# Middle experts of a mixture layer in pairs of PSUM banks: accumulation on TensorE, 768-column operations, differences read from PSUM

## The chip, the cores and the metric

One Trainium2 chip, of which the kernel uses one core. The metric is the device time of one execution in microseconds (us). Before the change it was 2509.31 us (median of three runs, 2509.23 to 2515.71). The core's engines work in parallel, each on its own queue in order: TensorE (PE) multiplies into PSUM, whose 2 KB banks hold 512 fp32 columns for each of 128 partitions; VectorE (DVE) and ScalarE (ACT) read and write PSUM and SBUF; GpSimd (POOL) works on SBUF alone; SyncE (SP) issues most transfers. They wait for each other by semaphores.

## The reference

Three stages follow one another, all in fp32: a linear attention, a soft mixture of eight experts over its 2304 tokens of width 512, and a second mixture that sends every token to one expert. The change is in the first mixture:

```
x: 2304 x 512      w1: 8 x 512 x 1024      w2: 8 x 1024 x 512
P = exp(x @ w_gate - max), then 8 rounds of normalising its rows and its columns
for e in range(8):
    h = maximum(x @ w1[e], 0)
    out += P[:, e:e+1] * (h @ w2[e])
```

## The kernel before, in words

Everything is kept transposed, features on partitions and tokens along the columns. A matmul's operand is split in a high part, rounded to a shorter mantissa, and the rest (tile[:, 0] and tile[:, 1]), and a product is made of high x high, high x rest and rest x high: three matmuls for each 128 rows (`product`, lines 412 to 417).

The hidden width of an expert is cut in halves, so there are 16 half experts n, and the tokens in three blocks bi of 768; `HS` lists the 48 pairs (n, bi) in the order in which they run, with the blocks up and down in turn, so that two neighbours of a change of n have the same tokens. Each pair, which the text calls a block, is a 2 x 2 by 2 x 2 block product for layer 1 (x by w1) and another for layer 2 (h by w2), over quarters of 384 tokens. Both are done by Strassen's scheme in Winograd's form, with 7 products in place of 8. In the code, S1 to S4 are the sums of weight quarters, T1 to T4 those of the moving side (of x, and of h in layer 2), A11 to A22 weight quarters, B11 to B22 moving ones. A product has two output halves j, of six matmuls of 128x384 each.

Blocks with n below 2 and with n = 15 run the seven products in layer 1 alone, and plain products in layer 2 (`p2_plain`). The 39 blocks with n from 2 to 14 (the mixed ones) run seven products in both.

Layer 1 (`p1_group`, line 491) goes through the seven products for j = 0 and then for j = 1, each into a bank of 384 columns: m = A11 B11 is copied to SBUF by ScalarE (`tu`), u = m + S2 T2 and v = u + S1 T1 (`tv`) are added by VectorE, S4 B22 goes into the same bank as S1 T1, and so on; each of the four results then goes through `put`. In a mixed block `put` is `strassen` (line 457): VectorE takes the maximum with 0 and multiplies by the gate, writing SBUF; then come the layer-2 sums T1 to T4 (`comb`, line 462), the high parts by ScalarE (`high`, line 428) and the rests (`rest`, line 431). For j = 0 the sums and rests are GpSimd's, for j = 1 VectorE's; all of these have their operands in SBUF. `later` delays some by a number of ticks. Layer 2 (`p2_strassen`, line 765) then runs S4, A11, S3, S1, S2, A12 and A22; behind each j of each product VectorE adds the bank to the block's running sum in SBUF (`acc`, line 768).

The order of the work is written out by hand. Each generator yields after a piece of some six matmuls; a yield is a tick, and `at_tick(h, i, fn)` hangs other work on tick i of block h: the seven reloads of the next block's x tiles (`xreload`, ticks 7 to 13), the load of the next gates (`load_gate`, tick 16) and, in the third block of a half expert, the preparation of the next half's weights (`wops`): two raw loads a layer, four sums of 128x512 on GpSimd, and for each of seven weights a high part by ScalarE (line 338) and a rest by GpSimd (line 339).

Of the kernel before, what the change touches and what calls it, by code (L numbers as in the profile page):

```python
# [25 lines left out]
P = 128  # L26
# [13 lines left out]
XUSE = ("B11", "T2", "T1", "B22", "T3", "B21", "T4")  # L40
# [5 lines left out]
def build(tc, a, out):  # L46
# [4 lines left out]
    pp = top.enter_context(tc.tile_pool(name="pp", bufs=1, space=PSUM))  # L51
# [39 lines left out]
    live = {}  # L91
# [327 lines left out]
    hb, pend = {}, deque()  # L419
    HN = {(0, 0): "B11", (0, 1): "T1", (1, 0): "B21", (1, 1): "B22"}  # L420

    def raw_h(nm, j):
        t = live["h3"].tile([P, TH], F32, tag="r" + {"B22": "T2", "B21": "T4"}.get(nm, nm), bufs=1 if nm in ("B11", "T3") else 2, name="r" + nm)
        hb["raw", nm, j] = t
        return t

    def high(nm, j, src=None):
        A.copy(hb[nm][:, 0, j], hb["raw", src or nm, j])  # L428

    def rest(nm, j, eng, src=None):  # L430
        eng.tensor_tensor(out=hb[nm][:, 1, j], in0=hb["raw", src or nm, j], in1=f32(hb[nm][:, 0, j]), op=ALU.subtract)  # L431

    def later(ticks, fn, *args):
        pend.append([ticks, partial(fn, *args)])

    def pending():
        for x in list(pend):
            x[0] -= 1
            if x[0] < 0:
                pend.remove(x)  # L440
                x[1]()
# [6 lines left out]
    def gate(nm, j, th, src):  # L448
        V.scalar_tensor_tensor(out=raw_h(nm, j), in0=src, scalar=0.0, in1=hb["gate"][:, th * TH:(th + 1) * TH], op0=ALU.max, op1=ALU.mult)  # L449

    def gated(hv, th, j, src):
        nm = HN[hv, th]
        gate(nm, j, th, src)
        high(nm, j)
        later(1, rest, nm, j, V if j else G)

    def strassen(hv, th, j, src):
        eng, dl = (V, 0) if j else (G, 2)

        def comb(out, x, y):  # L460
            o = hb["raw", out, j] if ("raw", out, j) in hb and out != "T3" else raw_h(out, j)
            eng.tensor_tensor(out=o, in0=hb["raw", x, j], in1=hb["raw", y, j], op=ALU.subtract)  # L462

        if (hv, th) == (0, 1):
            gate("T1", j, 1, src)
        elif (hv, th) == (1, 1):
            gate("T2", j, 1, src)
            high("B22", j, "T2")
            comb("T3", "T2", "T1")
            rest("B22", j, eng, "T2")  # L470
            later(dl, high, "T3", j)
            later(dl + 1, rest, "T3", j, eng)
        elif (hv, th) == (0, 0):
            gate("B11", j, 0, src)
            comb("T1", "T1", "B11")
            high("B11", j)
            comb("T2", "T2", "T1")
            rest("B11", j, eng)
            later(dl, high, "T1", j)
            later(dl + 1, rest, "T1", j, eng)  # L480
            later(dl, high, "T2", j)
            later(dl + 2, rest, "T2", j, eng)
        else:
            gate("T4", j, 0, src)
            high("B21", j, "T4")
            later(0, rest, "B21", j, eng, "T4")
            later(0, comb, "T4", "T2", "T4")
            later(dl + 1, high, "T4", j)
            later(dl + 2, rest, "T4", j, eng)

    def p1_group(n):
# [3 lines left out]
        put = plain if n < 2 else gated if n == NGR - 1 else strassen  # L495
        for nm in ("B11", "T1", "B21", "B22"):
            hb[nm] = hp.tile([P, 2, 2, TH], F32R, tag="h" + nm, name=f"h{nm}")
        if put is strassen:
            for nm in ("T2", "T3", "T4"):
                hb[nm] = live["h3"].tile([P, 2, 2, TH], F32R, tag="h" + nm, name=f"h{nm}")  # L500
        if n >= 2:
            hb["gate"] = gates.popleft()
        for j in range(2):
            b0 = psum("A", [P, TH])
            product(b0, 1, j, "A11", xs["B11"], True, True)
            tu = hp.tile([P, TH], F32, tag="tu", name="tu")
# [8 lines left out]
            tv = hp.tile([P, TH], F32, tag="tv", name="tv")  # L515
# [8 lines left out]
            add(tv, b2, tv)  # L524
            put(1, 1, j, tv)
# [239 lines left out]
    def p2_strassen(n, bi):  # L765
        def read(q_, j, ps, op=ALU.add):
            z = acc(bi)[:, q_, j]
            V.tensor_tensor(out=z, in0=z, in1=ps, op=op)  # L768

        Y = [psum("A", [P, TH]) for _ in range(2)]  # L770
        for k in range(2):
            for j in range(2):
                product(Y[j], 2, j, "S4", hb["B22"], True, True, (k,))
                if k:
                    read(1, j, Y[j], ALU.subtract)
            yield

        def both(banks, wn, hn, start, q_, op=ALU.add):
            for j in range(2):
                product(banks[j], 2, j, wn, hb[hn], start, True)  # L780
                read(q_, j, banks[j], op)
                yield

        X = [psum("D", [P, TH]) for _ in range(2)]
        yield from both(X, "A11", "B11", True, 0)
        yield from both(Y, "S3", "T3", False, 3)
        Z = [psum("A", [P, TH]) for _ in range(2)]
        yield from both(Z, "S1", "T1", True, 1)
        yield from both(X, "S2", "T2", False, 1)
        W_ = [psum("D", [P, TH]) for _ in range(2)]  # L790
        yield from both(W_, "A12", "B21", True, 0)
        yield from both(Z, "A22", "T4", False, 2, ALU.subtract)

# [223 lines left out]
    def pair(which, j, nm):  # L1017
# [12 lines left out]
    def wsplit(i, which, c):  # L1030
        r = rw[which][c]
        j = n_w[which] % 7
        n_w[which] += 1
        hi, lo = pair(which, j, f"{i}_{c}")
# [121 lines left out]
    SL15 = {"A21": "S3"}  # L1156
    for h, (n, bi) in enumerate(HS):
        nxt = HS[h + 1][1] if h + 1 < NH else bi
        if nxt != bi:
            if n:  # L1160
                for k in range(len(XUSE)):
                    at_tick(h, 7 + k, partial(xreload, nxt, k))
# [254 lines left out]
```

## Time and profile before

| | |
|---|---|
| median of three runs | 2509.31 us |
| the profiled execution, its span | 2515.74 us, 2513.9 us |
| PE busy | 2123.5 us (84%) |
| DVE busy | 1616.5 us (64%) |
| POOL busy | 1164.6 us (46%) |
| ACT busy | 857.3 us (34%) |
| mean granted TensorE clock | 0.925 |

The busy time of PE counts matmuls from start to modelled end, and they overlap, so it overstates how full TensorE is. The granted clock is a share of the full 2.4 GHz; it has two levels, 1.2 and 2.4 GHz, so a value between them is a mix over the stretch. In the rows below, psA and psD are PSUM banks, xB and xT the tiles of x, hB and hT those of the gated h, rB and rT their unsplit values, w1A to w2S the weights, acca and accb the running sums. L417 is line 417.

### The profile page before, as it was taken

The numbers are of one execution on the slowest core, as the hardware profiler recorded it, in microseconds if no ns is written. First come the engines' busy times: TensorE is split into PE (matmuls) and PEld (weight loads), VectorE is DVE, ScalarE is ACT, GpSimd is POOL, SyncE is SP. The second block draws the span as 40 slices with busy tenths as digits, with TensorE's granted clock in tenths as the row PEclk, the third lists the DMA queues.
The fourth block names the chain that finished last, engine by engine and source line by source line (L and its number), as shares of the span: only waits on it lengthen the run. The fifth ranks groups of instructions, "written<-read, shape, count | busy, mean of one in ns | idle before, by whom it ended". The sixth has DMA issues, their size and how long they took to land.

```text
span 2513.9 us, 32723 instructions
## 1 busy us (share of the span) xinstructions
PE 2123.5 (84%) x11627; PEld 1984.8 (79%) x11627; DVE 1616.5 (64%) x2740; ACT 857.3 (34%) x1625; POOL 1164.6 (46%) x1036
## 2 busy tenths in 40 slices
PE   9999999878787878787878787878787878689998
PEld 9998888778686868777777777878786878577887
DVE  6665454666666666666656665666666563459996
ACT  5564321222222222222222223131313122267776
POOL 1263223555555555546463637282827241126553
PEclk9999999998898989898989898989898988889999
DMA  3344533323232424151505141423333225535472
GB/s 114 116 161 156 205 124 112 128 95 134 99 141 91 162 75 171 64 197 32 205 24 205 39 190 60 169 79 149 115 114 132 98 97 123 92 51 176 160 244 101
DMA packets 128313, 314.43 MB, mean 125 GB/s; under 512 B 20856, under 2 KB 75272, under 8 KB 128146
## 3 DMA queue, kind: packets, MB, share of 16 engines
q1 hardware_dynamic: 124050, 301.79, 35.2%
q0 software_dynamic: 4096, 10.51, 1.5%
q8 instruction: 93, 1.52, 0.3%
q14 instruction: 74, 0.61, 0.1%
HBM read 335.78 MB, written 32.05 MB: 146 GB/s over the span
## 4 chain that ended last, share of the span: by engine, by line
PE 53%; DVE 23%; POOL 11%; ACT 4%; DMA 4%; issue 4%; SPq 1%; DVEq 0%; POOLq 0%; ACTq 0%
PE psA L415 10%; PE psA L417 8%; PE psA L416 8%; DVE rT L462 4%; DVE rT L449 4%; PE psD L415 3%; PE psD L417 3%; PE psD L416 3%; DVE hB L431 3%; DVE tv L493 3%; DVE psA L493 3%; POOL hT L431 2%; PE psD L200 2%; ACT hB L428 2%; DVE hT L431 2%
## 5 line engine op out<-in xcount | busy, mean ns | idle before, releaser
L462 POOL TENSOR_TENSOR rT<-rT,rT 128x384 f32<-128x384 f32 x117 | 118.8, 1015 | 687.8 <-DVE rT L449 681.7
L415 PE MATMUL psD<-hB,w2A 128*128 128x384 f32 x528 | 194.0, 367 | 93.2 <-ACT hB L428 73.2
L428 ACT CAST hT<-rT 128x384 fp32r<-128x384 f32 x318 | 161.4, 512 | 224.2 <-POOL rT L462 106.8
L415 PE MATMUL psA<-hT,w2S 128*128 128x384 f32 x312 | 138.1, 443 | 110.2 <-DVE acca L768 71.9
L431 POOL TENSOR_TENSOR hT<-rT,hT 128x384 fp32r<-128x384 f32 x159 | 194.3, 1246 | 53.6 <-ACT hT L428 53.6
L416 PE MATMUL psD<-hB,w2A 128*128 128x384 f32 x528 | 193.9, 367 | 22.5 <-DVE hB L431 22.5
L493 DVE TENSOR_TENSOR psA<-psA,tu 128x384 f32<-128x384 f32 x192 | 108.1, 563 | 150.6 <-PE psA L417 150.2
L415 PE MATMUL psA<-xT,w1S 128*128 128x384 f32 x576 | 195.4, 339 | 2.0 <-DVE hB L446 2.0
L417 PE MATMUL psA<-xT,w1S 128*128 128x384 f32 x576 | 194.2, 337 | 0.0
L416 PE MATMUL psA<-xT,w1S 128*128 128x384 f32 x576 | 193.9, 337 | 0.0
L428 ACT CAST hB<-rT 128x384 fp32r<-128x384 f32 x156 | 80.2, 514 | 332.9 <-DVE rT L449 332.9
L507 ACT COPY tu<-psA 128x384 f32<-128x384 f32 x96 | 45.7, 476 | 432.9 <-PE psA L417 432.7
L417 PE MATMUL psD<-hB,w2A 128*128 128x384 f32 x528 | 188.8, 358 | 0.0
L415 PEld LDWEIGHTS psD<-hB,w2A 128*128 128x128 f32 x528 | 108.0, 205 | 100.0 <-ACT hB L428 77.4
L415 PEld LDWEIGHTS psA<-hT,w2S 128*128 128x128 f32 x312 | 81.9, 263 | 125.1 <-DVE acca L768 81.6
L768 DVE TENSOR_TENSOR acca<-acca,psA 128x384 f32<-128x384 f32 x208 | 112.6, 551 | 93.0 <-PE psA L417 93.0
L493 DVE TENSOR_TENSOR tu<-psA,tu 128x384 f32<-128x384 f32 x96 | 53.5, 557 | 137.2 <-PE psA L417 76.6
L415 PE MATMUL psA<-xB,w1S 128*128 128x384 f32 x192 | 75.4, 393 | 77.5 <-DVE tv L493 74.5
L416 PEld LDWEIGHTS psD<-hB,w2A 128*128 128x128 f32 x528 | 108.0, 205 | 36.0 <-DVE hB L431 36.0
L416 PE MATMUL psA<-hT,w2S 128*128 128x384 f32 x312 | 133.1, 426 | 0.0
L417 PE MATMUL psA<-hT,w2S 128*128 128x384 f32 x312 | 131.8, 423 | 0.0
L415 PE MATMUL psA<-xB,w1A 128*128 128x384 f32 x384 | 130.6, 340 | 0.0
(372 smaller groups left out, 6795.7 us busy)
## 6 DMA issues: line engine op xcount, KB each, us to landing
xT<-xpd SPq DMA_DIRECT2D x120, 768.0 KB
rw<-in_moe_w SPq DMA_DIRECT2D x176, 512.0 KB
xB<-xpd SPq DMA_DIRECT2D x90, 768.0 KB
raw<-in_moe_w SPq DMA_DIRECT2D x34, 512.0 KB
gate<-gd SPq DMA_DIRECT2D x45, 384.0 KB
rx<-in_moe_w SPq DMA_DIRECT2D x30, 512.0 KB
xpd<-xT SPq DMA_DIRECT2D x12, 768.0 KB
xpd<-xB SPq DMA_DIRECT2D x9, 768.0 KB
```

What stands on the lines that cost most here:

```text
L200: T.matmul(ps[:, off:off + w], eq[:, sg, h_, ci * P:(ci + 1) * P], kvz[:, h_, sg, o:o + w], start=(sg == 0), stop=(sg == 1))
L415: T.matmul(bank, w[:, 0, j, k, :], x[:, 0, k, :], start=start and k == 0, stop=False, skip_group_check=True)
L416: T.matmul(bank, w[:, 0, j, k, :], x[:, 1, k, :], start=False, stop=False, skip_group_check=True)
L417: T.matmul(bank, w[:, 1, j, k, :], x[:, 0, k, :], start=False, stop=stop and k == 1, skip_group_check=True)
L428: A.copy(hb[nm][:, 0, j], hb["raw", src or nm, j])
L431: eng.tensor_tensor(out=hb[nm][:, 1, j], in0=hb["raw", src or nm, j], in1=f32(hb[nm][:, 0, j]), op=ALU.subtract)
L449: V.scalar_tensor_tensor(out=raw_h(nm, j), in0=src, scalar=0.0, in1=hb["gate"][:, th * TH:(th + 1) * TH], op0=ALU.max, op1=ALU.mult)
L462: eng.tensor_tensor(out=o, in0=hb["raw", x, j], in1=hb["raw", y, j], op=ALU.subtract)
L493: V.tensor_tensor(out=out, in0=x, in1=y, op=ALU.add)
L507: A.copy(tu, b0)
L768: V.tensor_tensor(out=z, in0=z, in1=ps, op=op)
```

## The change

The mixed blocks no longer run `p1_group` and `p2_strassen` but one generator, `layers`. It works on pairs of PSUM banks, Q0 to Q3, both j at once: the two j of a product go to the two banks of a pair, and every other operation takes the 768 columns of the pair. The running totals of layer 1 (m, u, v and v + S4 B22) are accumulated by the matmuls in one pair, with copies taken by ScalarE on the way. Gates and differences are computed in place in PSUM where they can be, and the differences left to GpSimd are five rests of 768 columns. The last product of layer 2, A22 by T4, runs in ticks 2 and 3 of the next block (`before`). A mixed block has 28 ticks. The reloads of x follow the order of use, the ticks of the weights' preparation are other ones, and the gates' load moves to tick 20. In the other blocks, `p1_group` writes one of its sums to PSUM instead of SBUF, and with n = 15 the rests are all VectorE's.

```
-XUSE = ("B11", "T2", "T1", "B22", "T3", "B21", "T4")
+XUSE = ("B11", "T2", "B21", "T1", "T3", "B22", "T4")
...
+    def psum_pool(name):
+        pst.close()
+        live["pp"] = pst.enter_context(tc.tile_pool(name=name, bufs=1, space=PSUM, reuse_waits="tile"))
...
     def gated(hv, th, j, src):
-        nm = HN[hv, th]
-        gate(nm, j, th, src)
-        high(nm, j)
-        later(1, rest, nm, j, V if j else G)
-
-    def strassen(hv, th, j, src):
...
+        t = hb[HN[hv, th]]
+        gate(src, th, src)
+        A.copy(t[:, 0, j], src)
+        V.tensor_tensor(out=t[:, 1, j], in0=src, in1=f32(t[:, 0, j]), op=ALU.subtract)
+
+    def pair(q_):
+        n_ps[0] += 1
+        return live["pp"].tile([P, 2, 512], F32, tag=f"Q{q_}", name=f"Q{q_}_{n_ps[0]}")[:, :, 0:TH]
+
+    def hraw(tag):
+        return live["h3"].tile([P, 2, TH], F32, tag="r" + tag, name="r" + tag)
+
+    def high(nm, src):
+        A.copy(hb[nm][:, 0], src)
+
+    def rest(nm, src, eng):
+        eng.tensor_tensor(out=hb[nm][:, 1], in0=src, in1=f32(hb[nm][:, 0]), op=ALU.subtract)
+
+    def twin(bank, kind, wn, x, start):
+        for j in range(2):
+            product(bank[:, j], kind, j, wn, x, start, True)
+            yield
+
+    def layers(h, n, bi):
+        odd = h % 2
+        qx, qz = (0, 3) if odd else (3, 0)
...
+        b0 = pair(qz)
+        yield from twin(b0, 1, "A11", xs["B11"], True)
+        m1c = hraw("a")
+        A.copy(m1c, b0)
+        yield
...
+        yield from twin(b0, 1, "S2", xs["T2"], False)
+        u2c = hp.tile([P, 2, TH], F32, tag="tu", name="u2c")
+        A.copy(u2c, b0)
+        b1 = pair(1)
+        yield from twin(b1, 1, "A12", xs["B21"], True)
+        tt(b1, b1, m1c, ALU.add)
+        r11 = hraw("b")
+        gate(r11, 0, b1)
+        high("B11", r11)
+        yield from twin(b0, 1, "S1", xs["T1"], False)
+        rest("B11", r11, G)
+        vc = hraw("c")
+        A.copy(vc, b0)
+        b2 = pair(2)
+        yield from twin(b2, 1, "S3", xs["T3"], True)
+        tt(b1, b2, vc, ALU.add)
+        r22 = hraw("d")
+        gate(r22, 1, b1)
+        high("B22", r22)
+        for i, _ in enumerate(twin(b0, 1, "S4", xs["B22"], False)):
+            if i == 0:
+                rest("B22", r22, G)
+            yield
+        gate(b0, 1, b0)
+        t3 = hraw("c")
+        tt(t3, r22, b0)
+        high("T3", t3)
+        tt(b0, b0, r11)
+        high("T1", b0)
+        for i, _ in enumerate(twin(b2, 1, "A22", xs["T4"], False)):
+            if i == 0:
+                rest("T3", t3, G)
+            yield
+        tt(b2, b2, u2c, ALU.add)
+        rest("T1", b0, V)
+        gate(b2, 0, b2)
+        high("B21", b2)
+        tt(r22, r22, b0)
+        high("T2", r22)
+        X = pair(qx)
+        for i, _ in enumerate(twin(X, 2, "A11", hx["B11"], True)):
+            if i == 0:
+                rest("T2", r22, G)
+            yield
+        Y = pair(1)
+        yield from twin(Y, 2, "S4", hx["B22"], True)
+        read(1, Y, ALU.subtract)
+        read(0, X)
+        rest("B21", b2, V)
+        Z = pair(qz)
+        yield from twin(Z, 2, "S1", hx["T1"], True)
+        t4 = hraw("a")
+        tt(t4, r22, b2)
+        high("T4", t4)
+        read(1, Z)
+        for i, _ in enumerate(twin(Y, 2, "S3", hx["T3"], False)):
+            if i == 0:
+                rest("T4", t4, G)
+            yield
+        read(3, Y)
+        yield from twin(X, 2, "S2", hx["T2"], False)
+        read(1, X)
+        W_ = pair(2)
+        yield from twin(W_, 2, "A12", hx["B21"], True)
+        read(0, W_)
+        yield
+        w22 = wt[2, "A22"]
+        yield from twin(Z, 2, w22, hx["T4"], False)
+        read(2, Z, ALU.subtract)
+        yield
...
-            add(tv, b2, tv)
-            put(1, 1, j, tv)
+            add(b1, b2, tv)
+            put(1, 1, j, b1)
...
-    def p2_strassen(n, bi):
...
+    XFREE = {"B11": (7, 1), "T2": (8, 5), "T1": (9, 9), "B22": (10, 13), "T3": (11, 11), "B21": (12, 7), "T4": (13, 15)}
...
+            if mixed(n):
+                ops_at(h, ((2, "A11"), (3, "S1r"), (4, "S3r"), (5, "S2r"), (8, "A12"), (9, "S4r"), (10, "S2"), (12, "S1"), (14, "S3"), (16, "S4"), (18, "A22 load")), o1)
...
-                ops_at(h, ((18, "A11"), (19, "S1r"), (20, "S3r"), (21, "S3 S2r"), (23, "S1"), (25, "S2"), (26, "A12"), (27, "S4r"), (40, "S4"), (42, "A22 load")), wops(2, n + 1))
+                ops_at(h, ((18, "A11"), (20, "S1r"), (21, "S3r"), (25, "S2r"), (40, "A12"), (41, "S4r"), (43, "S1"), (45, "A22"), (46, "S4"), (49, "S3"), (51, "S2 load")), o2)
...
-            at_tick(h, 16, partial(load_gate, HS[h + 1][0] // 2, nxt))
+            at_tick(h, 20, partial(load_gate, HS[h + 1][0] // 2, nxt))
...
+            gen = layers(h, n, bi)
+            for i in range(28 if mixed(HS[h + 1][0]) else 30):
+                if i == 2:
+                    next(gen)
+                if i not in (2, 3):
+                    next(gen)
+                elif before:
+                    next(before)
+                run_at(h, i)
+                if i == 3 and before:
+                    next(before)
+                if i == 27:
+                    next(gen)
+            before = gen
```

A tick of 40 and over belongs to the next block (51 is its tick 11). `read` adds a pair to a running sum, `tt` is an operation of two tensors on VectorE.

## Rows read from the trace of the kernel before

**Rows 1.** Windows: length, each engine's busy time (instructions), granted clock, DMA share, GB/s.

```profile
452.85:2043.87 1591.02, 1284.48 (x6553) 1214.66 (x6553) 1027.87 (x1681) 401.31 (x806) 834.79 (x713) 0.91 0.32 117
497.87:2043.87 1546.00, 1249.67 (x6385) 1181.42 (x6385) 996.51 (x1634) 391.39 (x786) 813.95 (x696) 0.91 0.32 116
985.69:1023.25 37.56, 32.17 (x169) 30.56 (x169) 24.53 (x43) 7.79 (x16) 11.77 (x11) 0.95 0.42 158
1023.25:1069.25 46.00, 33.63 (x169) 31.43 (x169) 29.40 (x43) 13.90 (x28) 34.17 (x28) 0.85 0.10 32
```

**Rows 2.** TensorE's waits, 497.8 to 2043.8: us in total, times, longest.

```profile
PE psD L415 <- ACT hB L428: 73.2, 13, 5.6
PE psA L415 <- DVE acca L768: 71.9, 26, 3.4
PE psA L415 <- DVE tv L493: 54.9, 72, 0.8
PE psA L416 <- DVE hB L431: 36.4, 38, 1.5
PE psA L415 <- DVE accb L768: 35.7, 12, 3.4
PE psD L416 <- DVE hB L431: 21.3, 38, 0.7
```

**Rows 3.** Timeline of TensorE: start us, duration us, what [idle before].

```profile
1011.12 0.45 PE L415 MATMUL psA<-hT,w2S 128*128 128x384 f32 x1 [2.51 <-DVE acca L768]
...
1013.06 0.53 PE L415 MATMUL psA<-hT,w2S 128*128 128x384 f32 x1
1013.38 0.53 PE L416 MATMUL psA<-hT,w2S 128*128 128x384 f32 x1
...
1017.01 0.33 PE L415 MATMUL psD<-hT,w2S 128*128 128x384 f32 x1
...
1023.25 0.33 PE L415 MATMUL psA<-xB,w1A 128*128 128x384 f32 x1
...
1025.16 0.33 PE L417 MATMUL psA<-xT,w1S 128*128 128x384 f32 x1
```

**Rows 4.** Windows of 5 us; columns as in rows 1.

```profile
1005.00:1010.00 5.00, 3.10 (x17) 2.46 (x15) 4.76 (x9) 2.05 (x4) 0.39 (x1) 1.00 1.01 416
1010.00:1015.00 5.00, 3.88 (x16) 3.88 (x17) 3.95 (x9) 0.51 (x1) 0.00 (x0) 0.75 0.44 149
1025.00:1030.00 5.00, 4.35 (x25) 4.03 (x25) 2.49 (x5) 0.00 (x0) 0.00 (x0) 1.00 0.00 0
```

**Rows 5.** Single lines: duration in ns, minimum, median and maximum; first and last start.

```profile
L736 DVE TENSOR_TENSOR acca<-acca,gate x4: 950/950/953, 414.4 to 423.2; 128x768 f32<-128x768 f32 x4
L376 DVE TENSOR_TENSOR xB<-xB x2: 2633/2651/2669, 256.5 to 296.8; 128x768 fp32r<-128x768 f32 x2
L768 DVE TENSOR_TENSOR acca<-acca,psA x208: 539/554/557, 522.7 to 2044.1; 128x384 f32<-128x384 f32 x104
L462 DVE TENSOR_TENSOR rT<-rT,rT x117: 557/1184/1650, 475.8 to 2027.0; 128x384 f32<-128x384 f32 x117
L375 ACT CAST xB<-xB x6: 830/832/835, 200.4 to 296.0; 128x768 fp32r<-128x768 f32 x6
L376 POOL TENSOR_TENSOR xT<-xshB,xT x4: 1817/1834/1844, 182.3 to 203.9; 128x768 fp32r<-128x768 f32 x4
L339 POOL TENSOR_TENSOR w1S<-raw,w1S x48: 1268/1284/1610, 144.8 to 2031.7; 128x512 fp32r<-128x512 f32 x48
```

**Rows 6.** Timeline of VectorE; columns as in rows 3.

```profile
422.33 1.82 DVE L736 TENSOR_TENSOR acca<-acca,gate 128x768 f32<-128x768 f32 x2
...
1025.60 0.56 DVE L493 TENSOR_TENSOR tu<-psA,tu 128x384 f32<-128x384 f32 x1 [1.59 <-PE psA L417]
...
1036.94 0.57 DVE L493 TENSOR_TENSOR psA<-psA,tu 128x384 f32<-128x384 f32 x1 [1.41 <-PE psA L417]
1037.55 0.56 DVE L449 SCALAR_TENSOR_TENSOR rT<-psA,gate 128x384 f32<-128x384 f32 x1
```

More of the change, by code (lines that the diff above doesn't have):

```diff
@@ L417, in product @@
             T.matmul(bank, w[:, 1, j, k, :], x[:, 0, k, :], start=False, stop=stop and k == 1, skip_group_check=True)
-    hb, pend = {}, deque()
+    hb = {}
     HN = {(0, 0): "B11", (0, 1): "T1", (1, 0): "B21", (1, 1): "B22"}
[L422 to L441, printed above, removed]
     def plain(hv, th, j, src):
@@ new lines, in hraw, with tt, read @@
+    def hraw(tag):
[11 more added lines that the diff above has]
+        qx, qz = (0, 3) if odd else (3, 0)
+        def tt(out, x, y, op=ALU.subtract):
+            V.tensor_tensor(out=out, in0=x, in1=y, op=op)
+        def read(q_, ps, op=ALU.add):
+            z = acc(bi)[:, q_]
+            V.tensor_tensor(out=z, in0=z, in1=ps, op=op)
+        b0 = pair(qz)
[3 more added lines that the diff above has]
+        yield
+        for nm in ("B11", "T1", "B21", "B22"):
+            hb[nm] = hp.tile([P, 2, 2, TH], F32R, tag="h" + nm, name=f"h{nm}")
+        for nm in ("T2", "T3", "T4"):
+            hb[nm] = live["h3"].tile([P, 2, 2, TH], F32R, tag="h" + nm, name=f"h{nm}")
+        hx = dict(hb)
+        hb["gate"] = gates.popleft()
+        yield from twin(b0, 1, "S2", xs["T2"], False)
[68 more added lines that the diff above has]
+        yield
@@ L763, in p2_plain @@
                     yield
-    def p2_strassen(n, bi):
[L766 to L792, printed above, removed]
     ohc = c0.tile([P, 7, E], BF16, name="ohc")
@@ L1015, in build, with places @@
     PAIRS = (("wS1_1", "wS2_1"), ("wS4_1", "wA12_1"), ("wA11_1", "wS3_1"))
-    def pair(which, j, nm):
+    def places(which, j, nm):
         if which == 1 and j < 4:
@@ L1033, in wsplit @@
         n_w[which] += 1
-        hi, lo = pair(which, j, f"{i}_{c}")
+        hi, lo = places(which, j, f"{i}_{c}")
         if (which, c) == (2, 3) and i > 1:
@@ L1160, in build @@
             if n:
-                for k in range(len(XUSE)):
-                    at_tick(h, 7 + k, partial(xreload, nxt, k))
+                for k, nm in enumerate(XUSE):
+                    at_tick(h, XFREE[nm][mixed(n)], partial(xreload, nxt, k))
             else:
@@ L1231, in build, with run_at @@
         at_tick(NH - 2 + k // 40, k % 40, fn)
+    def run_at(h, i):
+        for fn in sched.pop((h, i), ()):
+            fn()
+    before = None
     for h, (n, bi) in enumerate(HS):
-        gen, tick = (p1_group(n), 0) if h else (first, filled[0])
-        second_layer = p2_plain if n < 2 or n == NGR - 1 else p2_strassen
-        for part in (gen, second_layer(n, bi)):
-            for _ in part:
-                pending()
-                for fn in sched.pop((h, tick), ()):
-                    fn()
-                tick += 1
+        if mixed(n):
+            if before is None:
+                psum_pool("pq")
+            gen = layers(h, n, bi)
[12 more added lines that the diff above has]
+            before = gen
+            if not mixed(HS[h + 1][0]):
+                next(gen)
+                psum_pool("pr")
+        else:
+            gen, tick = (p1_group(n), 0) if h else (first, filled[0])
+            for part in (gen, p2_plain(n, bi)):
+                for _ in part:
+                    run_at(h, tick)
+                    tick += 1
     assert not sched, sched.keys()
-    assert not pend
     def prime(i):
@@ L1343, in build @@
         second(NALW, NBLK)
+    pst.close()
     top.close()
```

64 lines of the change are left out of this document (19 added, 45 removed).

## The prediction

> **What bounds the kernel now.** I read the windows first, then TensorE's waits, then the timelines. 39 of the 48 blocks are mixed (experts' halves 2 to 14 by three token blocks) and take 1591.0 of the 2513.9 us [rows 1]; almost all the change lies there. An ordinary one takes 37.5 us and the third of each half, which also prepares the next weights, 46 to 47 [rows 1]. A block issues 168 matmuls (the window's 169 counts one cut by its edge). At full clock one starts every 173 ns: 36 of them lie between 1017.01 and 1023.25 [rows 3]. So a block needs 29.12 us of TensorE, and six matmuls, which I call a slot, 1.04 us. The 38 blocks of the window 497.87:2043.87 need 1106.6 of its 1546.0 us. TensorE's six largest waits there add to 293.4 us [rows 2], and the 146 us left are the price of the slow clock: after an idle stretch of 2.5 us the matmuls come every 0.32 us for some 3 us, and the granted clock of that window is 0.75 [rows 3, 4].
>
> The waits have three places. At the change from layer 1 to layer 2, hB and hT wait for differences on VectorE and GpSimd (73.2, 36.4 and 21.3), longest in third blocks, where GpSimd is busy 34.2 of 46.0 us. The write-back of the S4 product is read late by VectorE (acca, accb: 71.9 and 35.7). And in layer 1 the S4 product waits for VectorE to read S1's (tv: 54.9).
>
> **The change, part by part.** The numbers of matmuls stay. Layer 1 runs by pairs, so every dependent product has a whole other product, two slots or 2.08 us, between it and its reader, and the last layer-2 product (A22 by T4) runs in slots 2 and 3 of the next block. VectorE, per mixed block: 43 operations of 384 columns (10 additions, 8 gates, 11 differences, 14 write-backs) become 20 of 768, all with one operand in PSUM. GpSimd: 11 of 384 become 5 of 768. ScalarE: 16 of 384 become 10 of 768.
>
> Prices. No VectorE operation of 768 columns with a PSUM operand is in the trace. The nearest rows of its width are 0.95 us (starts 0.87 apart, as two take 1.82) and 2.65 us, both with SBUF operands alone; the 384-column write-back from PSUM takes 0.54 to 0.56 and never more [rows 5, 6]. Two of those, 1.11, is one end, 0.87 the other, 2.65 the far end. I take 0.95, with 0.87 from start to start, because the operations with a PSUM operand never stretched while the ones between SBUF tiles did. ScalarE 0.83, GpSimd 1.83 for 768 columns and 1.28 for a weight of 512 [rows 5]; dear ends for GpSimd: the weight row's longest, 1.61, and by columns 2.4. VectorE starts 0.27 after the slot that it waits for (1025.16 + 0.17, then 1025.60), and an operation that reads the one before starts 0.05 after its end [rows 3, 6].
>
> *Layer 1.* S4 may start when ScalarE has copied v out of its pair. From the end of A12: addition at 0.27, gate to 2.2, high part of B11 to 3.1, copy to 3.9; S4 is due at 4.16. Nothing waits, with 0.3 to spare. In a third block a weight's copy stands ahead on ScalarE: 0.25 late. The first copies of m and u have 2.08 us of cover and take 0.83.
>
> *Layer change.* Zero is the end of S4 by B22. VectorE: gate in PSUM 0.27 to 1.22, T3 to 2.22, T1 to 3.09, v21 to 3.96; ScalarE's high of T1 to 3.97; rest of T1 4.02 to 4.97, gate to 5.84, T2 to 6.71. TensorE meanwhile has A22 by T4 (layer 1), A11 by B11 and S4 by B22, six slots or 6.24 us, whose operands are ready earlier (rest of B22 on GpSimd by 2.9). Z takes the pair that T2 reads, so S1 by T1 starts at 6.76: 0.5 late. Behind it S3 needs Y read (7.6 against 8.8), S2 needs T2's rest on GpSimd (9.4 against 10.9) and X read (8.5), A12 needs B21's rest (9.4 against 13). Bounds of this wait: 0, and 2.0 at 1.11 us an operation. An ordinary block: 29.12 + 0.5 = 29.6 us.
>
> *Layer 2 to layer 1.* T4's difference, high and rest end near 15, and it is due at 17.2, behind the next block's first product. The 2.5 us idle of this place goes, and with it the slow stretch behind it; next late is T2's last read above.
>
> *Third blocks.* GpSimd's queue, from the block's first matmul: the first weight's rest cannot start before 3.8, and the A12 rest waits behind ScalarE's high of B11 from about 8.9 to 12. Up to the end of T4's rest there follow 14 weight operations and 5 differences: 3.8 + 3.1 + 14 x 1.28 + 5 x 1.83 = 34.0. TensorE wants T4's low part at 29.12 + 2.08 + 0.17 and what it is late by then (0.25, 0.25 for B22's rest, 0.5): 32.4. So 1.6 late, and 2.1 more than an ordinary block in all. Bounds: 0, and some 8.5 with the dear prices (3.8 + 2 + 14 x 1.61 + 5 x 2.4 = 40.3, so 8 late). The seven weight operations left run in the next block's first twelve slots, 9 us before its own differences need GpSimd.
>
> *Transfers.* The seven x tiles of 768 KB are now asked for in order of use in slots 1 to 15 instead of 7 to 13, each behind its last product, so SP does not wait out of order. An ordinary block moves 37.56 x 158 GB/s = 5.9 MB; in 29.6 us that is 200 GB/s, and the queues reach 416 [rows 1, 4]. The gates' load goes to slot 20, behind the two raw loads, which wait for A22's rest on GpSimd; it lands some 8 us before its first use. If that cover went, the gate (and S4 behind it) would be late by what is missing. I take 0; bounds 0 and 2 us in third blocks.
>
> *Edges and plain blocks.* The first mixed block took 45.0 (1591.0 - 1546.0), 7.5 above the ordinary; VectorE's late start there is now hidden by eight slots, so I keep 4. At the end the last A22 by T4 has no cover, and the PSUM pool changes: 4. In nine other blocks one addition goes to PSUM instead of SBUF, and in three of them 12 differences move from GpSimd to VectorE (12 x 0.55 = 6.6): 0, bounds -3 and +7.
>
> *Sum.* 13 x (3 x 29.6 + 2.1) + 8 = 1190 in place of 1591: 401 less. The profiled execution took 2515.7 (its span 2513.9), so 2115; its median is 2509.3, 6.4 lower, and the runs fall on both values. I take the middle, 2112.
>
> **Rivals.** *The side engines at the dear ends.* 13 x (3 x 31.1 + 8.5) + 8 = 1331: 2253. For it: third blocks leave GpSimd no slack. Against it: its long rows are those beside VectorE operations between SBUF tiles, which the mixed blocks no longer have.
>
> *The clock does not come back.* TensorE still has two or three short waits in a block. If they cost what the slow clock costs now, 146/38 = 3.8 us a block, the time is 2112 + 39 x 3.8 = 2260. Against it: the window 1025:1030 has two such waits (4.35 of 5 us busy) and a granted clock of 1.00 [rows 4]; only the long idle stretch brought 0.75. The Trainium skill ("TensorE: Matmul & The Clock Gate", section "A second HAM failure mode: psum-queue depth-cycling") says that cycling through PSUM banks makes TensorE idle briefly between groups of matmuls so often that its clock oscillates. By that rule it would be this rival, since every product of the change waits on a reader of its pair. The trace so far shows the fall only behind the long idle stretch, not behind short ones.
>
> *VectorE becomes the bound (slower).* Should its 768-column operations run as the xB row did, 2.65 us, 20 of them make 53 us a block: 39 x 53 in place of 1591, or 2990. It decides from 2.04 us an operation, where 20 make the present mean of 40.8. For it: it is a row of this width on this engine. Against it: both its inputs were in SBUF, and GpSimd ran too.
>
> *The change does not do what it says*, that the products serialise on their pairs, is contained in the first two: the waits that it adds are those of the readers.
>
> **How the numbers follow.** My forecast 0.62 (2065 to 2170: from 39 x 29.12 + 3 to 1.4 us more a block); dear ends 0.17; clock 0.12; slower 0.08; no change 0.01. The range 2065 to 2235 takes in half and more of the two middle rivals and leaves out the rest of them, the slow one and what falls below 2065: some 2 in 10. About 0.3% is what a measurement of this kernel can tell from none. Faster 0.91, same 0.01, slower 0.08.
>
> **What would show it.** A regular pattern of two blocks of 29 to 30.5 us and one of 31 to 33; a granted clock over 0.97 in the mixed stretch; VectorE rows of 768 columns at 0.93 to 0.97; TensorE's largest waits at S1 by T1 for VectorE's T2, and at the carried A22 by T4 for GpSimd. A third block over 36 us, or a VectorE row over 1.1, would make the prediction wrong.

## The result, and the profile after

The changed kernel takes 2121.52 us (median of four runs, 2115.75 to 2125.39), 0.844 of the time before (2511.55 us, now the median of four runs), with a 95% interval of 0.842 to 0.847. The forecast was 2112, the range 2065 to 2235. Of the profiled executions, 2125.4 stands against 2515.7.

The page after, its busy engines and the slices with the granted clock (tenths of full speed):

```profile
PE 2004.9 (94%) x11627; PEld 1905.9 (90%) x11627; DVE 1316.3 (62%) x1855; ACT 867.0 (41%) x1391; POOL 1033.8 (49%) x790
...
PEclk9999999999999999999999999999999988799999
```

Windows after: the mixed blocks, the 37 of them that the waits below cover, three neighbours (the block behind a third one, an ordinary one, a third one), and all that follows. Columns as in [rows 1].

```profile
454.27:1646.78 1192.51, 1159.56 (x6552) 1132.52 (x6552) 721.45 (x784) 411.83 (x572) 717.02 (x480) 1.00 0.46 156
485.68:1614.38 1128.70, 1099.23 (x6218) 1074.54 (x6217) 678.09 (x740) 388.85 (x538) 670.88 (x449) 1.00 0.47 158
...
1003.78:1035.53 31.75, 29.97 (x170) 29.04 (x170) 18.33 (x20) 10.79 (x15) 20.85 (x14) 1.00 0.69 229
1035.53:1065.27 29.74, 29.36 (x170) 29.07 (x170) 18.33 (x20) 8.08 (x10) 9.23 (x5) 1.00 0.59 199
1065.27:1095.33 30.06, 29.85 (x170) 29.00 (x169) 18.33 (x20) 12.86 (x19) 25.10 (x19) 1.00 0.12 40
...
1646.78:2123.60 476.82, 418.17 (x2084) 362.76 (x2084) 338.29 (x492) 258.91 (x376) 159.85 (x152) 0.92 0.49 137
```

The mixed stretch fell from 1591.0 [rows 1] to 1192.5 us at a granted clock of 1.00 (0.91 before). What stands ahead of it is 1.4 us longer and what follows 6.8 (476.8 against 2513.9 - 2043.9 = 470.0): 398.5 - 1.4 - 6.8 = 390.3, the whole difference of the two executions. VectorE runs 20 instructions in a block of 29.74 us where it ran 43 in 37.56, and is busy for 18.3 us instead of 24.5.

TensorE's waits from 485.7 to 1614, which answer to [rows 2]:

```profile
PE Q L422 <- POOL hT L456: 16.3, 12, 1.4
PE Q L421 <- ACT hB L453: 9.7, 25, 0.6
PE Q L422 <- POOL hB L456: 2.5, 12, 0.2
PE Q L421 <- ACT rc L498: 0.4, 1, 0.4
```

They add to 28.9 us in 37 blocks, where the largest six added to 293.4 in 38. The 37 blocks need 37 x 29.12 = 1077.4 of the 1128.7 us; the other 22.4 I put down to the refill behind each wait (after the one that ends at 1054.79 the next matmul starts 0.25 us later instead of 0.17), which no row adds up. No part of this stretch ran at the lower clock. What was left over by the same reckoning before, 146 us, was more than the slow clock: of the matmuls between 497.87 and 2043.87 of that trace, 507 are followed by the next only after 0.30 us or more with no wait between, which at 0.173 each is some 80 us too many. The rest of the 146 lies mostly, like the 22.4, around the waits.

The two waits that count lie where the prediction put them. First S1 by T1 in an ordinary block, TensorE, then VectorE, then ScalarE (start, duration):

```profile
1054.07 0.34 PE L423 MATMUL Q<-hB,w2S 128*128 128x384 f32 x1
1054.79 0.41 PE L421 MATMUL Q<-hT,w2S 128*128 128x384 f32 x1 [0.38 <-ACT hB L453]
```

```profile
1051.96 0.96 DVE L456 TENSOR_TENSOR hT<-Q,hT 128x768 fp32r<-128x768 f32 x1
1052.83 0.96 DVE L437 SCALAR_TENSOR_TENSOR Q<-Q,gate 128x768 f32<-128x768 f32 x1
1053.70 0.94 DVE L468 TENSOR_TENSOR rd<-rd,Q 128x768 f32<-128x768 f32 x1
```

```profile
1053.88 0.80 ACT L453 CAST hB<-Q 128x768 fp32r<-128x768 f32 x1 [1.95 <-DVE Q L437]
```

VectorE's T2 (rd<-rd,Q) ends at 1054.64, ScalarE's high of B21 (hB<-Q) at 1054.68, and TensorE starts at 1054.79, 0.55 behind the even pace. The profile names ScalarE, which ended last; the two ends are too near to tell them apart by the trace. Second, the carried A22 by T4 behind a third block, GpSimd and then TensorE:

```profile
1092.52 1.28 POOL L350 TENSOR_TENSOR ws<-rx,rx 128x512 f32<-128x512 f32 x1
1093.88 1.29 POOL L350 TENSOR_TENSOR rx<-rx,rx 128x512 f32<-128x512 f32 x1
1095.14 1.81 POOL L456 TENSOR_TENSOR hT<-ra,hT 128x768 fp32r<-128x768 f32 x1
```

```profile
1097.00 0.44 PE L422 MATMUL Q<-hT,w2A 128*128 128x384 f32 x1 [1.34 <-POOL hT L456]
```

T4's rest stands behind two sums of weights, for a product much further ahead.

### The profile page after: what moved, and what is told of

Its sections match the earlier page's. It is cut to its first block, busy times and chain, and to the rows that moved or that the text cites. A ratio compares the mean times of both kernels' runs of the same rounds, so it can differ in the third digit from the quotient of the medians.

```text
span 2123.6 us, 31194 instructions
## 1 busy us (share of the span) xinstructions
PE 2004.9 (94%) x11627; PEld 1905.9 (90%) x11627; DVE 1316.3 (62%) x1855; ACT 867.0 (41%) x1391; POOL 1033.8 (49%) x790
## 4 chain that ended last, share of the span: by engine, by line
PE 61%; DVE 14%; POOL 10%; issue 6%; ACT 4%; DMA 4%; SPq 0%; DVEq 0%; ACTq 0%; POOLq 0%
PE Q L421 11%; PE Q L422 10%; PE Q L423 10%; PE psD L206 3%; POOL w1S L345 3%; DVE Q L468 2%; POOL hT L456 2%; DVE Q L437 2%; PE psD L421 2%; PE psD L423 2%; PE psD L422 2%; PE psA L421 2%; POOL w1A L345 2%; PE psD L1135 1%; PE psD L1133 1%
## 5 line engine op out<-in xcount | busy, mean ns | idle before, releaser
L472 DVE TENSOR_TENSOR acca<-acca,Q 128x768 f32<-128x768 f32 x182 | 170.3, 950 | 157.9 <-PE Q L423 157.9
L421 PE MATMUL Q<-hT,w2S 128*128 128x384 f32 x468 | 159.5, 341 | 10.0 <-ACT hB L453 10.0
L421 PE MATMUL Q<-xT,w1S 128*128 128x384 f32 x468 | 156.4, 334 | 0.9 <-ACT ra L477 0.9
L422 PE MATMUL Q<-hT,w2S 128*128 128x384 f32 x468 | 156.6, 335 | 0.0
L423 PE MATMUL Q<-hT,w2S 128*128 128x384 f32 x468 | 156.5, 334 | 0.0
L423 PE MATMUL Q<-xT,w1S 128*128 128x384 f32 x468 | 156.4, 334 | 0.0
L422 PE MATMUL Q<-xT,w1S 128*128 128x384 f32 x468 | 156.3, 334 | 0.0
L472 DVE TENSOR_TENSOR accb<-accb,Q 128x768 f32<-128x768 f32 x91 | 85.0, 950 | 84.4 <-PE Q L423 84.4
L1072 DVE TENSOR_TENSOR s1l<-rw,s1h 128x1024 fp32r<-128x1024 f32 x88 | 103.4, 1226 | 23.9 <-ACT s1h L1071 23.2
L1072 DVE TENSOR_TENSOR s2l<-rw,s2h 128x1024 fp32r<-128x1024 f32 x76 | 100.3, 1366 | 9.4 <-ACT s2h L1071 9.4
L421 PEld LDWEIGHTS Q<-hT,w2S 128*128 128x128 f32 x468 | 87.8, 188 | 19.8 <-ACT hB L453 19.5
L421 PE MATMUL Q<-xB,w1A 128*128 128x384 f32 x312 | 104.3, 334 | 0.7 <-DVE accb L824 0.7
L456 POOL TENSOR_TENSOR hT<-rd,hT 128x768 fp32r<-128x768 f32 x39 | 72.3, 1853 | 66.2 <-ACT hT L453 66.2
L422 PE MATMUL Q<-xB,w1A 128*128 128x384 f32 x312 | 104.2, 334 | 0.0
L423 PE MATMUL Q<-xB,w1A 128*128 128x384 f32 x312 | 104.2, 334 | 0.0
L421 PE MATMUL Q<-hB,w2A 128*128 128x384 f32 x312 | 104.2, 334 | 0.0
L423 PE MATMUL Q<-hB,w2A 128*128 128x384 f32 x312 | 104.2, 334 | 0.0
L422 PE MATMUL Q<-hB,w2A 128*128 128x384 f32 x312 | 104.2, 334 | 0.0
```

Of the source, the lines that this page charges most:

```text
L421: T.matmul(bank, w[:, 0, j, k, :], x[:, 0, k, :], start=start and k == 0, stop=False, skip_group_check=True)
L422: T.matmul(bank, w[:, 0, j, k, :], x[:, 1, k, :], start=False, stop=False, skip_group_check=True)
L423: T.matmul(bank, w[:, 1, j, k, :], x[:, 0, k, :], start=False, stop=stop and k == 1, skip_group_check=True)
L456: eng.tensor_tensor(out=hb[nm][:, 1], in0=src, in1=f32(hb[nm][:, 0]), op=ALU.subtract)
```

## The experiments

All differ from the changed kernel in the edit shown. The mixed stretch and single blocks are from each run's profile; a ratio is to the kernel before, timed beside it, with its 95% interval. Blocks are given in the order: behind a third one, ordinary, third (31.7, 29.7 and 30.1 us in the changed kernel).

**T2 ahead of the gate of h21.**

```
+        tt(r22, r22, b0)
+        high("T2", r22)
         gate(b2, 0, b2)
         high("B21", b2)
-        tt(r22, r22, b0)
-        high("T2", r22)
```

> One move in the changed kernel: the difference T2 (the last read of the pair that layer 2's S1 product takes over) is issued ahead of the gate of h21 and of ScalarE's high part of B21. Theory 1: the 0.55 us that TensorE loses before S1 by T1 in two of three mixed blocks is its wait for VectorE's T2. Then T2 ends 0.87 us earlier, the wait goes, the ordinary blocks take 29.2 us instead of 29.74 and 30.04, and the whole is 14 us shorter (26 blocks x 0.55), about 2107 where the changed kernel is 2121. Theory 2: the releaser that the profile names, ScalarE's high of B21, is the real one. Then that now ends 0.87 us later, the wait grows to some 1.4 us, and the whole is about 22 us longer, 2144.

Measured: ratio 0.837 (0.834 to 0.839), median 2104.0, mixed stretch 1175.4, 17.2 shorter.

```profile
812.39:843.59 31.20, 29.69 (x170) 29.05 (x170) 18.25 (x20) 10.79 (x15) 20.95 (x15) 1.00 0.72 236
843.59:872.71 29.12, 29.12 (x170) 29.12 (x170) 18.24 (x20) 8.09 (x10) 9.23 (x5) 1.00 0.63 203
872.71:902.64 29.93, 29.70 (x170) 29.06 (x169) 18.34 (x20) 12.87 (x19) 24.96 (x19) 1.00 0.12 37
```

The ordinary block is down to 29.12 us, TensorE's own columns to the hundredth. ScalarE's high of B21 now comes later and nobody waits for it: VectorE's read was the cause, and the releaser that the profile named was not. The block behind a third one fell by 0.55 as well, but the third one by 0.13 only (30.06 to 29.93), where theory 1 had 29.2: it had been waiting elsewhere already, for GpSimd's rest of B22.

**Two weight sums behind T4's rest.**

```
-(18, "A11"), (20, "S1r"), (21, "S3r"), (25, "S2r"), ...
+(18, "A11"), (23, "S1r"), (24, "S3r"), (25, "S2r"), ...
```

> One move in the changed kernel: in the third block of a half expert two weight sums on GpSimd (S1 and S3 of layer 2) go from ticks 20 and 21 to 23 and 24, behind T4's rest instead of ahead of it; the work is the same. Theory 1: the 31.7 us of the block behind (against 29.7) is TensorE's wait of 1.4 us and its refill for T4's rest, which stands in GpSimd's queue behind weight work. Then T4's rest ends 2.6 us earlier, the 31.7 become 29.8, and the whole is 13 x 1.9 = 25 us shorter, about 2097. Theory 2: GpSimd is full in that stretch, and what is put back (the S weights of layer 2, first used in slot 18 of the next block) becomes the new wait: the whole stays within 6 us of 2121.

Measured: ratio 0.839 (0.835 to 0.842), median 2107.3, mixed stretch 1172.6, 19.9 shorter; the block behind a third one takes 30.07 instead of 31.75.

```profile
811.80:841.87 30.07, 29.67 (x169) 29.06 (x169) 18.34 (x20) 10.89 (x15) 20.89 (x15) 1.00 0.76 247
```

Theory 1: GpSimd was not full, its order was wrong. The saving is 1.65 a block and not 1.9: that is the whole of the wait and its refill. The 0.3 us that stay against an ordinary block are at S4 by B22 of layer 1, where ScalarE copies a weight before it copies v (`rc`). The prediction had this wait of 0.25 in third blocks; the block behind one has it too.

```profile
821.03 0.62 ACT L344 CAST w2S<-rx 128x512 fp32r<-128x512 f32 x1
821.55 0.79 ACT L498 COPY rc<-Q 128x768 f32<-128x768 f32 x1
```

**The carry undone.** The generator of a block runs to its end before the next begins:

```
-            for i in range(28 if mixed(HS[h + 1][0]) else 30):
+            before = gen
+            for i in range(30):
                 if i == 2:
                     next(gen)
                 if i not in (2, 3):
                     next(gen)
-                elif before:
-                    next(before)
                 run_at(h, i)
-                if i == 3 and before:
-                    next(before)
                 if i == 27:
                     next(gen)
-            before = gen
+            next(gen)
             if not mixed(HS[h + 1][0]):
-                next(gen)
                 psum_pool("pr")
```

> One part of the change undone: the last product of layer 2 (A22 by T4) stays in its own block, in slots 28 and 29, and is not carried behind the next block's first product. Theory 1: what the carry covers in an ordinary block is only ScalarE's copy of m between A11 and S2 on the same pair, since T4 is ready by then: a wait of 1.2 us a block (0.3 from TensorE to ScalarE, 0.8 the copy, 0.1 back), and in third blocks about 1 us more for T4's rest: 39 x 1.25 + 13 x 1 = 62 us more, about 2183, clock still at 1.00 in the mixed blocks. Theory 2: the carry is what removed the 2.5 us wait and the slow clock behind it at the end of the old block: then each block loses 2.5 us and the 3.8 us of the slow clock again, 39 x 6 = 245 us, about 2365.

Measured: ratio 0.880 (0.877 to 0.883), 2215 us, mixed stretch 1281.6, 89.1 longer. TensorE's waits over the mixed blocks:

```profile
PE Q L422 <- POOL hT L456: 41.3, 13, 3.4
PE Q L421 <- ACT ra L477: 36.1, 38, 1.2
```

The ordinary block takes 30.99, 1.25 more, with the wait for the copy of m (ra) that theory 1 named; the 2.5 us idle does not come back, so theory 2 fell. But third blocks take 36.0 on the average, 6 more and not 2. There T4's rest is 3.38 us late, and behind that wait the clock falls, as the windows of that place and of the same wait in the changed kernel show (the first two are without the carry):

```profile
937.53:942.53 5.00, 4.55 (x27) 4.22 (x25) 2.79 (x4) 0.98 (x2) 4.92 (x5) 1.00 0.57 171
942.53:947.53 5.00, 2.07 (x7) 2.07 (x8) 0.36 (x1) 0.02 (x1) 5.00 (x4) 0.82 0.70 120
```

```profile
1095.00:1100.00 5.00, 3.66 (x21) 3.35 (x20) 0.76 (x1) 1.94 (x3) 4.92 (x5) 1.00 0.47 151
```

**The carry undone, with T4's rest earlier** (both edits above), to see whether that is all that third blocks lost.

> The changed kernel without the carry, and with the two weight sums behind T4's rest. Without the carry alone, the blocks took 31.7, 31.0 and 36.0 us (31.7, 29.7 and 30.1 with it) and 2215 in all. Theory 1: of that, the wait for ScalarE's copy of m costs 1.25 us in every block, and the rest is T4's rest late by 3.4 us in third blocks, with a slow clock behind it. With T4's rest 2.6 us earlier, third blocks fall to about 32, the clock stays at 1.00, and the mixed stretch is near 39 x 31.1 = 1215, the whole 2150. Theory 2: third blocks lose for another reason that the carry covered (the weights' copies on ScalarE, or the next block's start): they stay at 35 or above and the whole above 2195.

Measured: ratio 0.859 (0.856 to 0.861), 2162 us, mixed stretch 1233.2, blocks 31.3, 31.0 and 32.5, clock 1.00. Theory 1: T4's late rest and the clock behind it made up most of the surplus. The mixed stretch is 18 us above the sum, and third blocks, where T4's rest is still up to 0.9 late, make nearly all of it. Against the kernel with the same order on GpSimd and the carry (1172.6), the carry is worth 60.6 us, 1.55 a block: the copy of m, and that 0.9 for T4 in third blocks.

**Differences between SBUF tiles again.**

```
-        gate(b0, 1, b0)
+        r01 = hraw("a")
+        gate(r01, 1, b0)
...
-        gate(b2, 0, b2)
+        r20 = hraw("b")
+        gate(r20, 0, b2)
...
```

and r01, r20 in place of b0, b2 in the differences and high parts.

> One part of the change undone: the gated h12 and h21 are written to SBUF instead of back into PSUM, so that six of VectorE's 20 operations of a mixed block (T3, T1, rest of T1, T2, rest of B21, T4) have both operands in SBUF; number, width and order are the same. Theory 1: such operations stretch while GpSimd reads SBUF (2.65 us for 768 columns in the kernel before, 0.95 beside an idle GpSimd). Four of them lie in the chain that ends with T2, so S1 by T1 is 3 to 6 us late in every block, and the clock may fall behind it: 39 x 3 to 39 x 8 more, 2240 to 2430. Theory 2: the gain is the width and the order, not where the operands lie: within 10 us of 2121.

Measured: ratio 0.880 (0.877 to 0.883), 2215 us, mixed stretch 1279.8, 87.3 longer, blocks 32.2, 31.1 and 35.1. VectorE and then GpSimd in an ordinary block, and GpSimd in a third one:

```profile
890.79 2.55 DVE L468 TENSOR_TENSOR rc<-rd,ra 128x768 f32<-128x768 f32 x1
893.37 0.96 DVE L468 TENSOR_TENSOR ra<-ra,rb 128x768 f32<-128x768 f32 x1
...
895.23 1.78 DVE L456 TENSOR_TENSOR hT<-ra,hT 128x768 fp32r<-128x768 f32 x1
...
897.80 0.94 DVE L468 TENSOR_TENSOR rd<-rd,ra 128x768 f32<-128x768 f32 x1
```

```profile
890.68 1.85 POOL L456 TENSOR_TENSOR hB<-rd,hB 128x768 fp32r<-128x768 f32 x1 [2.34 <-ACT hB L453]
894.34 1.85 POOL L456 TENSOR_TENSOR hT<-rc,hT 128x768 fp32r<-128x768 f32 x1 [1.81 <-issue]
```

```profile
922.45 2.01 POOL L345 TENSOR_TENSOR w1S<-raw,w1S 128x512 fp32r<-128x512 f32 x1
924.42 2.53 POOL L456 TENSOR_TENSOR hB<-rd,hB 128x768 fp32r<-128x768 f32 x1
```

Theory 1 in kind: the same operations stretch from 0.95 to 2.55 and 1.78 (T3, rest of T1), and in third blocks GpSimd's from 1.28 to 2.01 and from 1.84 to 2.53. In the ordinary block GpSimd kept its 1.85, and both VectorE operations that met it ended 0.81 and 0.82 us behind its end, whenever they had begun: they look like waiting for their turn rather than running slowly. Not in size: in an ordinary block GpSimd runs only five operations, so two of the four in the chain met one, and the wait is 1 us, not 3 to 6. Third blocks, where GpSimd runs most of the time, lose 5. The Trainium skill ("SBUF — State Buffer", section "Who interferes with whom") says that a VectorE instruction with two SBUF inputs contends with a GpSimd instruction that reads SBUF, and one with at most one, outside VectorE's 2-port performance modes, does not. These rows agree: the operation at 894.25, with one SBUF input, kept its 0.96 beside GpSimd.

Third blocks also show what the clock adds. Each of the 13 has a wait of 2.15 us for a rest of GpSimd; behind 8 of these the clock fell, behind 5 it did not, and nothing in the program tells them apart. One of each:

```profile
611.04:646.72 35.68, 31.84 (x169) 30.56 (x169) 21.49 (x20) 12.29 (x18) 28.65 (x19) 0.95 0.08 26
709.38:743.50 34.12, 30.30 (x170) 29.02 (x170) 21.47 (x20) 12.30 (x18) 27.18 (x18) 1.00 0.06 17
```

**VectorE in halves of 384 columns.** In `tt`, `gate`, `rest` and `read`:

```
-            V.tensor_tensor(out=out, in0=x, in1=y, op=op)
+            for j in range(2):
+                V.tensor_tensor(out=out[:, j], in0=x[:, j], in1=y[:, j], op=op)
```

> One size of the changed kernel: VectorE's 20 operations of 768 columns in a mixed block become 40 of 384, in the same order and with the same operands; ScalarE and GpSimd keep their 768. Theory 1 (readers only have to end inside the products between): two starts of 384 columns take 0.94 us against 0.87 for one of 768, so VectorE's chain from S4 to T2 is some 0.2 us longer, which may be given back because each half can start when the half before it is done; the blocks stay within 0.3 us of 31.7, 29.7 and 30.0, the whole within 10 us of 2121. Theory 2: the width of VectorE's operations is where the gain comes from (VectorE's busy time fell from 24.5 to 18.3 us a block): then the halves give 1 us or more a block back, 2160 or above.

Measured: ratio 0.858 (0.857 to 0.860), 2163.1 us, mixed stretch 1226.9, 34.3 longer, blocks 32.0, 30.9 and 31.3; S1 by T1 waits 1.45 us.

```profile
875.45 1.17 DVE L474 TENSOR_TENSOR Q<-Q,rb 128x384 f32<-128x384 f32 x2
876.53 1.16 DVE L474 TENSOR_TENSOR Q<-Q,u2c 128x384 f32<-128x384 f32 x2
877.59 1.01 DVE L459 TENSOR_TENSOR hT<-Q,hT 128x384 fp32r<-128x384 f32 x2
```

Theory 1 fell: I had two starts at 0.94. That holds for halves that write SBUF (1.01 for two). Two that write the same pair in PSUM take 1.16 or 1.17, the second starting only when the first has ended. The chain gets 1 us longer and TensorE pays it: width matters where it lengthens the chain that TensorE waits for.

**Rests of the last half expert one step later.** In `gated`, the rest is kept, and `late()` issues it behind the next gate:

```
         A.copy(t[:, 0, j], src)
-        V.tensor_tensor(out=t[:, 1, j], in0=src, in1=f32(t[:, 0, j]), op=ALU.subtract)
+        late()
+        hb["late"] = partial(V.tensor_tensor, out=t[:, 1, j], in0=src, in1=f32(t[:, 0, j]), op=ALU.subtract)
```

> One edit outside the mixed blocks of the changed kernel: in the three blocks of the last half expert each rest is issued on VectorE behind the next gate instead of straight behind ScalarE's high part that it reads. Theory 1: the 4 us that the first of these blocks lost (36.7 to 40.6) are VectorE standing 0.6 us before each rest until ScalarE has the high part, so that the sum that layer 1's S4 product waits for comes 2 us late and the clock falls behind it: that block goes back to 36.5 to 38, the whole is 3 to 5 us shorter, 2117. Theory 2: the loss is VectorE's four rests more a block (2.2 us, GpSimd's before): then the block stays at 40 or above and the whole at 2121.

Measured: the block takes 37.56 us instead of 40.64, clock 1.00 instead of 0.92; the whole, ratio 0.843 (0.841 to 0.844), cannot be told from the changed kernel. What follows that block takes 434 to 446 us in the eleven profiles of the changed kernel and its variants (below).

Theory 1 holds for the wait: VectorE's pauses of 0.55 to 0.60 us before each rest are gone, and S4 waits 0.65 us where it waited 2.04 with a slow stretch behind it, while another product now waits 1.71 for a deferred rest. But part of the 3.1 us is luck. The first wait of the block, 2.7 us, is the same in both kernels, and in the changed one the clock fell behind it, here it did not (windows of 5 us about its end, changed kernel first). With the same edit and the two moves below the clock fell there again, and the block took 38.86.

```profile
1651.78:1656.78 5.00, 3.90 (x14) 3.90 (x15) 2.18 (x4) 0.32 (x1) 0.00 (x0) 0.66 0.00 0
1646.17:1651.17 5.00, 3.90 (x22) 3.90 (x23) 3.50 (x7) 0.69 (x2) 0.00 (x0) 1.00 0.00 0
```

**The moves together.** First T2 and the weight sums as above; then with the deferred rests of the last half expert too; then also with the rest of one more weight (S2 of layer 1) behind B22's on GpSimd:

```
-(10, "S2"), (12, "S1"), (14, "S3"), ...
+(12, "S1"), (13, "S2"), (14, "S3"), ...
```

> The two moves that shortened the changed kernel together: T2's difference ahead of the gate of h21, and the two weight sums behind T4's rest. If the two waits lie in different blocks and places, the savings add (17 and 20 us in the mixed stretch): blocks of 29.5, 29.1 and 29.9 us, the mixed stretch 1155, the whole 2086. If one uncovers the other, as T2's earlier end did not shorten the third block by more than 0.15, the whole stays at 2095 or above.

> The two moves in the mixed blocks and the deferred rests of the last half expert together. If all three are separate waits: the mixed stretch 1155 us, the first block of the last half expert 37 instead of 40.6, the whole 2082. If the deferred rests gain nothing: as the kernel with the two moves alone.

> The best kernel so far (T2 earlier, two weight sums behind T4's rest, deferred rests in the last half expert), with the rest of weight S2 behind B22's rest on GpSimd (tick 13 instead of 10). Theory 1: what third blocks still lose (29.93 us against 29.12) is mostly S4 by B22 waiting for B22's rest, 0.22 us and the refill behind it. Then they take 29.5, 13 x 0.45 = 6 us less: 2076 where the best is 2082. Theory 2: GpSimd's queue is full there and the next rest (T3 or T2) is late instead: third blocks stay at 29.9 or above.

Measured: the two moves alone 0.831 (0.829 to 0.832), 2092.3 us; with the deferred rests 0.827 (0.825 to 0.828), 2082.1 us; with the weight's rest moved as well 0.827 (0.825 to 0.830), 2080.7 us. The first two savings add: mixed stretches of 1154.2 and 1154.0, blocks of 29.4, 29.1 and 29.9. Windows of the second of the three, three neighbours and the mixed stretch:

```profile
806.66:836.09 29.43, 29.40 (x170) 29.08 (x169) 18.25 (x20) 10.90 (x15) 20.98 (x15) 1.00 0.79 253
836.09:865.21 29.12, 29.12 (x170) 29.12 (x169) 18.24 (x20) 8.08 (x10) 9.23 (x5) 1.00 0.64 203
865.21:895.14 29.93, 29.69 (x169) 29.05 (x169) 18.34 (x20) 12.87 (x19) 25.04 (x18) 1.00 0.13 36
451.43:1605.39 1153.96, 1147.63 (x6552) 1134.18 (x6552) 719.44 (x784) 413.13 (x571) 718.42 (x480) 1.00 0.49 161
```

39 x 29.12 is 1135.7, so 18 us are left in the mixed blocks. The last move brought third blocks to 29.83, between the two theories, with a wait of 0.13 for the next rest of GpSimd (T3's) as theory 2 had it, and no time that can be measured in the whole. Whether the deferred rests are worth the 10 us between the first two is open. In the profiles, the three blocks that they touch take, up to their last layer-2 matmul, 177.2 us instead of 183.1, 1.7 of it in the first; but these blocks take 179.3 to 188.6 in the eight profiles without the deferral, and 185.3 in the one with it alone.

## Why the prediction was right

*The floor.* The whole sum stood on TensorE's pace of 29.12 us a block, and the ordinary block takes exactly that in the kernel with T2 moved, and again in the one with all three moves.

*The layer change.* Forecast: S1 by T1 0.5 late behind VectorE's T2. Measured 0.55, and shown by the move of T2. VectorE's 768 columns took 0.94 to 0.97 us against 0.95. An ordinary block was forecast at 29.6 and took 29.74.

*Layer 2 to layer 1.* The step said that T4 is ready well before its product and that the 2.5 us of idle go; both are so, but the idle was not at this place. It stands in the middle of layer 2, ahead of S3 by T3, which waited for VectorE's write-back of S4's product [rows 3]. At the change to the next block TensorE ran on without a gap in the kernel before:

```profile
1023.08 0.33 PE L417 MATMUL psA<-hT,w2A 128*128 128x384 f32 x1
1023.25 0.33 PE L415 MATMUL psA<-xB,w1A 128*128 128x384 f32 x1
```

So the carry did not remove it, and without the carry it stays away. What fits is a clause of the layer change, "S3 needs Y read (7.6 against 8.8)": in the changed kernel VectorE has read S4's pair out 1.4 us before S3 by T3 begins, though no run undoes this alone:

```profile
1054.56 0.94 DVE L472 TENSOR_TENSOR acca<-acca,Q 128x768 f32<-128x768 f32 x1
1056.94 0.33 PE L421 MATMUL Q<-hT,w2S 128*128 128x384 f32 x1
```

What the carry covers was named only in passing, as the copies' cover of 2.08 us; undone, that copy is the 1.25 us that every block loses.

*Third blocks.* T4's rest was forecast 1.6 late and was 1.34; three neighbours together 90.9 and 91.55.

*The clock.* The rival did not come: 1.00 over the whole mixed stretch, with waits of 0.38 and 1.34 in it. Its price was too high, since it took all of the 146 us for the clock: at 80 us it is 2.1 a block, and the rival's time some 2195. The Trainium skill ("TensorE: Matmul & The Clock Gate", section "A second HAM failure mode: psum-queue depth-cycling") reports of a bf16 kernel that cycles through PSUM banks that its clock oscillated; no mixed block of the changed kernel shows that.

*Transfers.* No wait for a transfer is among the waits of the mixed blocks, and the blocks with reloads move 199 to 229 GB/s where 200 was forecast.

*What was mis-sized.* The edges: 8 forecast. The first mixed block takes 31.4, so about 2 in place of 4; at 91.55 for three blocks the 39 make 1190.1, and 2.4 of the 1192.5 are left for both ends. "In three of them 12 differences move from GpSimd to VectorE: 0, bounds -3 and +7": the stretch behind the mixed blocks is 6.8 longer, 4 of it in the first such block (36.7 to 40.6). In that block it is not only the differences' own time, as the prediction had it: VectorE stood still for ScalarE before each, and the clock fell behind two waits. Deferring the rests gave 3.1 back, of which 1.3 is the clock that did not fall behind a wait that the edit leaves alone. Mixed stretch and edges together were 1190 in the forecast and 1192.5 measured; that they agree so closely is luck in part, as the blocks took 8 us more than forecast and the edges 6 less. The other 8 us by which the profiled execution missed its 2115 lie outside the mixed blocks.

Where the 398.5 us came from: some 80 from the clock and most of the rest from waits and the refill behind them, by the rows. By undoing one thing at a time: the carry 89 (61 with GpSimd in the better order), the operands in PSUM 87, VectorE's width 34. These overlap (the first two share T4's late rest and the clock behind it), and even added they are 210 of the 398.5. What the accumulation on TensorE is worth by itself was not tried, nor the new order of the reloads and of the weights' preparation.

## What to carry to other kernels

Put a whole product between a matmul group and the next one that needs its reader's result, and then count only the longest chain on the reading engine: here seven operations against six slots. A short wait costs its length and a refill; a long one can cost the clock behind it as well (third blocks without the carry: 32.5 us with T4's rest earlier, 34.95 in the one block where the clock held, 36 where it fell), so the longest wait goes first. When two releasers end within a tenth of a microsecond, reorder them to learn which one is real.

## What the runs showed of the hardware

Operations between SBUF tiles on VectorE and GpSimd lengthen each other: VectorE's from 0.95 to 2.55 us in an ordinary block, where GpSimd kept its 1.85, and GpSimd's from 1.84 to 2.53 in third ones, for 768 columns. With one operand of VectorE's in PSUM both keep their time side by side, as in the changed kernel:

```profile
1049.20 0.95 DVE L468 TENSOR_TENSOR rc<-rd,Q 128x768 f32<-128x768 f32 x1
1049.15 1.85 POOL L456 TENSOR_TENSOR hB<-rd,hB 128x768 fp32r<-128x768 f32 x1 [2.34 <-ACT hB L453]
```

The clock does not fall behind every long wait of TensorE: behind equal waits of 3.4 us it fell 11 times of 12, behind equal ones of 2.15 us 8 times of 13, each within one execution. None of the waits of up to 1.4 us in the mixed blocks of the changed kernel brought it down.

Two VectorE operations that write halves of one PSUM pair in place take 1.17 us, two that write SBUF 1.01; no run shows whether the chip or the dependencies of the program set that. The stretch behind the mixed blocks takes 474 to 486 us in eleven profiles with nearly the same program there; the cause is open. It is noise in every comparison of whole times above; the mixed stretches do not contain it.
